# Four places back: a wait on an earlier landing for each opening load of a retention and feed-forward kernel

## The chip, the cores and the metric

The kernel runs on one core of one Trainium2 chip. The metric is the device time of one execution in microseconds (us), as the median of several runs. A core has TensorE (PE, the matmul engine), VectorE (DVE), ScalarE (ACT), GpSimd (POOL) and SyncE (SP). Each has its own queue and works it off in order; SP computes nothing here and issues most of the transfers. Sixteen DMA engines, shared by all queues, move data between the chip's memory (DRAM) and the core's on-chip memory.

## The reference

A recurrent retention layer over 4 batches, 8 heads, 768 positions and a head width of 64 feeds a two-layer perceptron:

```python
for t in range(S):
    state = gamma * state + outer(k[t], v[t])      # per batch and head, 64 x 64
    y[t] = scale * (q[t] @ state)
x = y, with the heads side by side                 # [3072, 512]
h = x @ w_in                                       # w_in [512, 2048]
g = max(h, 0) + alpha * min(h, 0)
out = g @ w_out                                    # w_out [2048, 512]
```

The decay gamma is a constant of each head. Inputs and output are float32.

## The kernel before

The kernel does the recurrence in chunks. A window w is 256 positions of four heads, and `place(w)` gives its batch, heads and positions; for each window k, q and v are loaded as tiles `ks`, `qs` and `vs` of 128 partitions by 512 elements, 256 KB each. `prep` scales k and q by powers of the decay into fp16 (`kdq`, L211, on DVE for the first windows and on POOL for later ones), `turn` transposes them on PE and copies them with ACT (L259, L265), `scores` and `masked` make the products within a chunk and mask them, `state_sums` makes the sums k·v that go into the state (L312), and `finish` writes the retention's output, transposed, into `xT`. v is cast to fp16 into `vx`, by ACT (L248) or POOL (L246).

The feed-forward part works on blocks of 512 positions. `ffn1` multiplies `xT` by w_in, in halves of 256 positions at first (L763) and then in wholes (L783); ACT and DVE apply the activation (L736, L725). `ffn2` multiplies by w_out (L809). Both weights come in pieces of 256 KB through the same buffers as k, q and v: `fetch` issues the load (L183) and `cast_w` casts a piece to fp16 on POOL (L188). In the first block, `tick` advances `ffn1` by a few matmuls at a time between the steps of the retention.

The whole order is written out by hand (a manual schedule): the order of the calls is the order on each engine, and waits are derived from which tile an instruction reads or overwrites. `behind(later, earlier, why)` adds a wait by hand.

What matters here is the opening, L1025 to L1089. ACT issues two small transfers (`tab`, 48 KB, and `alpha`, 8 KB). SP issues everything else in this order:

1. k and q of window 0, k and q of window 1, v of window 0, k and q of window 2, v of window 1, k and q of window 3, v of window 2 (L1027, eleven loads through L152);
2. the first piece of w_in, then v of window 3, then eleven more pieces of w_in (L1029 to L1033);
3. after the opening's instructions: the last four pieces of w_in, k, q and v of windows 4 and 5 among the sixteen pieces of w_out, and further windows.

The loads of 1 and 2 are 24 in number, go to buffers that nothing has used yet, and so wait for no other engine. The one thing that a load waits for is the counter that tells of landings: the build gives the DMAs eight counters in turn, so a load waits for the one eight places back in the list of all DMAs.

On POOL the order is: the scalings of windows 1 (q), 2 and 3, the cast of v of window 2, w_in's first piece, the cast of v of window 3, then the other pieces of w_in as they come, the scalings of window 4, and the pieces of w_out. On PE the opening begins with matmuls on a tile of ones (`busy`, L239, the `fill` of `turn` and `scores`) that compute nothing that is used.

Of the kernel before, what the change touches and what calls it, by code (L numbers as in the profile page):

```python
# [19 lines left out]
def kernel(  # L20
# [16 lines left out]
    nc = tc.nc  # L37
# [88 lines left out]
    def behind(later, earlier, why):  # L126
        tc.add_manual_dep(
            later.ins,
            earlier.ins.name,
            mybir.DependencyInfo(mybir.DependencyClass.Sync, mybir.DependencyReason.DATA),  # L130
            reason=why,
        )
# [7 lines left out]
    def place(w):  # L140
        u, g = divmod(w, 2)
        b, c3 = divmod(u, NUS)
        return u, g, b, c3

    def load(w, which="kqv"):
        u, g, b, c3 = place(w)
        t = staged.setdefault(w, {})
        for nm in which:
            src = {"k": k, "q": q, "v": v}[nm]
            t[nm] = sbp.tile([128, 4, 2 * D], FP, tag=f"{nm}s", bufs=8, name=f"{nm}s{w}")  # L150
            if w < NPE:
                nc.sync.dma_start(  # L152
                    out=t[nm],
                    in_=src[b, 4 * g : 4 * g + 4, TU * c3 : TU * c3 + TU, :].rearrange(
                        "h (p a) d -> p h (a d)", a=2
                    ),
                )
            else:
                at = TU * c3 + 128 * g
                nc.sync.dma_start(  # L160
                    out=t[nm].rearrange("p a (b d) -> p (a b) d", b=2),
                    in_=src[b, :, at : at + 128, :].rearrange("h p d -> p h d"),
                )
# [3 lines left out]
    def fetch(which, i, j):  # L167


        nm = "kqv"[len(pieces) % 3]  # L170
        t = sbp.tile([128, 4, 2 * D], FP, tag=f"{nm}s", bufs=8, name=f"{which}{i}_{j}")
        t = t.rearrange("p a b -> p (a b)")
        if which == "wo":
            src, dst = wo[:, 4 * i + j, :], w_out_all[:, 4 * i + j, :]
        elif i:
            s = slice(512 * i, 512 * i + 512)
            src, dst = wi[:, j, s], w_in_all[:, j, s]
        else:
            x, y = divmod(j, 2)
            at = slice(2 * y, 2 * y + 2), slice(256 * x, 256 * x + 256)  # L180
            src, dst = wi[:, at[0], at[1]], w_in_all[:, at[0], at[1]]
            t = t.rearrange("p (a b) -> p a b", a=2)
        nc.sync.dma_start(out=t, in_=src)  # L183
        pieces[which, i, j] = dst, t

    def cast_w(which, i, j):
# [800 lines left out]
    def tick(gen, m):  # L987
# [4 lines left out]
    wi = moe_w_in.rearrange("(hp p) d -> p hp d", p=128)  # L992
# [4 lines left out]
        out=ident,  # L997
        in_=ident,
# [6 lines left out]
    for i in range(2):  # L1005
        rows = slice(64 * i, 64 * i + 64)
        nc.gpsimd.affine_select(
            out=mask[rows].rearrange("p (a b j) -> p a b j", a=2, b=2),
            in_=ones[rows, 0:256].rearrange("p (a b j) -> p a b j", a=2, b=2),
# [7 lines left out]
            out=mask64[rows],  # L1017
            in_=ones[rows, 0:64],
# [6 lines left out]
    nc.scalar.dma_start(out=tab, in_=tab_h.ap())  # L1025
    nc.scalar.dma_start(out=alpha_sb, in_=moe_alpha.rearrange("(ft p) -> ft p", p=128))
    for w, which in ((0, "kq"), (1, "kq"), (0, "v"), (2, "kq"), (1, "v"), (3, "kq"), (2, "v")):  # L1027
        load(w, which)
    for i in range(3):  # L1029
        for j in range(4):  # L1030
            fetch("wi", i, j)
            if (i, j) == (0, 0):
                load(3, "v")  # L1033
    nc.vector.memset(warm, 0.0)
    nc.vector.memset(word, 0.0)
    nc.scalar.activation(out=warm, in_=warm, func=RELU, bias=0.0, scale=-1.0)
# [11 lines left out]
        out=oma_sb, in0=aps[:, 0:NFT], scalar1=-1.0, scalar2=1.0, op0=MULT, op1=ADD  # L1048
# [41 lines left out]
    for j in range(4):  # L1090
        fetch("wi", 3, j)
    load(4, "kq")
    for i in range(4):
        if i == 1:
            load(5, "kq")
        for j in range(4):
            if (i, j) == (1, 3):
                load(5, "v")
            fetch("wo", i, j)
        if i == 0:  # L1100
            load(4, "v")
# [14 lines left out]
    held = []  # L1116
# [115 lines left out]
```

## Time and profile before

| what | value |
|---|---|
| median of 3 runs | 199.52 us (198.75 to 199.85) |
| the profiled execution | 199.03 us, span 197.3 us |
| granted TensorE clock | 1.0 |
| PE busy | 191.6 us, 97% of the span |
| DVE, POOL, ACT busy | 76%, 58%, 50% |
| transfers, whole span | 38.21 MB, mean 194 GB/s |
| share of the chain that ended last by SP's queue and DMA | 4% and 3% |

The span is what the profiler saw between the first and the last instruction; the device time has some 1.7 us more around it. The page also cuts the span into 40 slices of 4.93 us. In the first nine slices, 44 us, the DMA engines are busy nearly throughout (the digits are tenths, the second row is what was moved):

```profile
DMA  5999999998899966999999999931072010400014
GB/s 163 318 345 371 357 348 382 402 343 186 192 215 232 238 154 157 317 325 233 219 178 230 240 322 236 219 75 41 3 212 56 0 56 3 161 0 3 0 56 159
```

A load's time to landing is counted from the start of its issue on SP to the moment at which all its DMA engines have told the counter that their part is there.

### The profile page before, as it was taken

To read this page: it belongs to the slowest core of one execution; us is meant where nothing else is said; L and a number is where in the kernel's file an instruction comes from. 1 tells how busy PE (TensorE), PEld (TensorE's weight loads), DVE (VectorE), ACT (ScalarE), POOL (GpSimd) and SP (SyncE) were. 2 spreads that over 40 slices of the span, in tenths; PEclk is the share of its full clock that TensorE was granted. 3 is DMA by queue.
4 is the path that set the end of the run, shared out by engine and by line. 5 is a ranking of instruction groups with operands and counts; after the bars stand their busy time and mean duration, and the time that the engine had idled before them with its cause. 6 is when DMAs were issued, how large, how long until landed. Compare 5 with 4: busy or idle time off the path is not lost.

```text
span 197.3 us, 6153 instructions
## 1 busy us (share of the span) xinstructions
PE 191.6 (97%) x2555; PEld 124.6 (63%) x2555; DVE 150.1 (76%) x251; ACT 97.9 (50%) x167; POOL 114.6 (58%) x153
## 2 busy tenths in 40 slices
PE   6989999999999999999999999999999999999993
PEld 2666545556885455444788644798544888448892
DVE  2585888564889956998995788995988964788962
ACT  3585765336686232477543276443376352566310
POOL 3489895856699991579892499381492091400011
PEclk9999999999999999999999999999999999999999
DMA  5999999998899966999999999931072010400014
GB/s 163 318 345 371 357 348 382 402 343 186 192 215 232 238 154 157 317 325 233 219 178 230 240 322 236 219 75 41 3 212 56 0 56 3 161 0 3 0 56 159
DMA packets 90476, 38.21 MB, mean 194 GB/s; under 512 B 68288, under 2 KB 85840, under 8 KB 90448
## 3 DMA queue, kind: packets, MB, share of 16 engines
q1 hardware_dynamic: 89856, 37.43, 71.5%
q8 instruction: 20, 0.33, 0.7%
q10 hardware_dynamic: 592, 0.39, 0.7%
q14 instruction: 8, 0.07, 0.1%
HBM read 27.32 MB, written 6.29 MB: 170 GB/s over the span
## 4 chain that ended last, share of the span: by engine, by line
PE 90%; SPq 4%; DMA 3%; issue 0%; POOL 0%; DVE 0%
PE hps L783 35%; PE ops L892 25%; PE ops L809 14%; PE hps L763 7%; SPq L152 4%; DMA vs<-in_v_dram 3%; PE y L614 2%; PE sc L638 1%; PE sums L652 1%; PE y L590 1%; PE trb L259 1%; PE y L392 1%; PE y L372 0%; PE sc L455 0%; SPq L183 0%
## 5 line engine op out<-in xcount | busy, mean ns | idle before, releaser
L725 DVE SCALAR_TENSOR_TENSOR gt<-hm,oma,hps 128x512 f16<-128x512 f32 (+1 forms) x112 | 73.0, 670 | 12.6 <-ACT hm L736 4.8
L736 ACT ACTIVATE hm<-hps 128x512 f32<-128x512 f32 x96 | 57.2, 597 | 32.5 <-PE hps L783 28.7
L783 PE MATMUL hps<-xT,win 128*128 128x512 f16 (+1 forms) x340 | 70.3, 366 | 0.0
L783 PEld LDWEIGHTS <-win 128*128 128x128 f16 x340 | 33.2, 98 | 35.2 <-DVE gt L725 0.4
L809 PE MATMUL ops<-wout,gt 128*128 128x512 f16 x128 | 29.3, 379 | 0.0
L913 POOL TENSOR_TENSOR c<-c,u 128x512 f32<-128x512 f32 x4 | 5.1, 1273 | 40.1 <-ACT c L908 22.1
L892 PEld LDWEIGHTS <-s 128*128 128x128 f16 x272 | 25.1, 98 | 2.8
L201 POOL TENSOR_TENSOR kdq<-ks,tab 128x256 f16<-128x256 f32 x32 | 19.0, 618 | 11.3 <-DMA ks<-in_k_dram 9.7
L948 POOL TENSOR_TENSOR s<-gt,s 128x1024 f16<-128x1024 f16 x6 | 13.8, 2310 | 13.1 <-PE sums L652 9.0
L892 PEld LDWEIGHTS <-gt 128*128 128x128 f16 x192 | 18.5, 98 | 2.9
L809 PEld LDWEIGHTS <-gt 128*128 128x128 f16 x128 | 11.9, 98 | 13.2
L201 POOL TENSOR_TENSOR kdq<-qs,tab 128x256 f16<-128x256 f32 x32 | 19.5, 632 | 0.0
L892 PE MATMUL ops<-wout,s 128*128 128x256 f16 (+1 forms) x136 | 15.3, 266 | 0.0
L892 PE MATMUL ops<-wout,gt 128*128 128x256 f16 x128 | 15.3, 273 | 0.0
L763 PE MATMUL hps<-xT,win 128*128 128x256 f16 x128 | 15.2, 273 | 0.0
L892 PE MATMUL ops<-t,s 128*128 128x256 f16 (+1 forms) x136 | 14.6, 266 | 0.0
L695 DVE TENSOR_TENSOR m<-sc,mi 128x1024 f16<-128x1024 f32 x8 | 9.8, 1220 | 4.7 <-PE sc L638 4.7
L763 PEld LDWEIGHTS <-win 128*128 128x128 f16 x128 | 12.0, 98 | 2.0
L828 ACT ACTIVATE os<-ops 128x512 f32<-128x512 f32 x8 | 4.7, 596 | 16.0 <-PE ops L809 14.7
L188 POOL CAST wout<-wo 128x512 f16<-128x512 f32 x16 | 10.5, 672 | 2.8 <-DMA wo<-in_moe_w_out_dram 2.7
L265 ACT ACTIVATE kq<-trb 128x512 f16<-128x512 f16 (+1 forms) x12 | 8.6, 736 | 4.8 <-PE trb L259 4.7
L231 POOL CAST vx<-vs 128x512 f16<-128x512 f32 x16 | 10.2, 639 | 0.6 <-DMA vs<-in_v_dram 0.6
(93 smaller groups left out, 217.7 us busy)
## 6 DMA issues: line engine op xcount, KB each, us to landing
ks<-in_k_dram SPq DMA_DIRECT2D x24, 256.0 KB, 4.6
qs<-in_q_dram SPq DMA_DIRECT2D x24, 256.0 KB, 4.6
vs<-in_v_dram SPq DMA_DIRECT2D x24, 256.0 KB, 4.5
wi<-in_moe_w_in_dram SPq DMA_DIRECT2D x16, 256.0 KB, 5.5
wo<-in_moe_w_out_dram SPq DMA_DIRECT2D x16, 256.0 KB, 5.5
out_dram<-c SPq DMA_DIRECT2D x11, 256.0 KB, 2.3
out_dram<-os SPq DMA_DIRECT2D x8, 256.0 KB, 3.9
out_dram<-y SPq DMA_DIRECT2D x3, 256.0 KB, 3.4
```

Source lines behind the costliest of these rows:

```text
L188: nc.gpsimd.tensor_copy(out=dst, in_=t)
L201: eng.tensor_tensor(out=kdq[:, kind, 2 * i : 2 * i + 2].rearrange("p x r d -> p r x d"), in0=src[:, 2 * i : 2 * i + 2].rearrange("p r (x d ...
L231: nc.gpsimd.tensor_copy(out=vx, in_=v_in)
L265: nc.scalar.activation(out=kq.rearrange("p b i -> p (b i)")[:, cols], in_=trb[:, cols], func=COPY, bias=0.0, scale=1.0,)
L695: nc.vector.tensor_tensor(out=m2.rearrange("p (s i) -> p s i", i=64), in0=sc.rearrange("p (s i) -> p s i", i=64), in1=mask64.unsqueeze(1). ...
L725: nc.vector.scalar_tensor_tensor(out=gt[:, ft, lo : lo + hps.shape[1]], in0=hm, scalar=oma_sb[:, ft : ft + 1], in1=hps, op0=MULT, op1=ADD,)
L736: nc.scalar.activation(out=hm, in_=hps, func=RELU, bias=0.0, scale=-1.0)
L763: nc.tensor.matmul(out=bank[:, 256 * x : 256 * x + 256], lhsT=w_in_all[:, hp, 128 * ft : 128 * ft + 128], rhs=tokens[:, hp // 2, 2 * t : 2 ...
L783: nc.tensor.matmul(out=hps[:, 128 * at.start : 128 * at.stop], lhsT=w_in_all[:, hp, 128 * ft : 128 * ft + 128], rhs=tokens[:, hp // 2, at, ...
L809: nc.tensor.matmul(out=opss[tq], lhsT=gt[:, ft, 128 * tq : 128 * tq + 128], rhs=w_out_all[:, ft, at], start=(ft == 0), stop=(ft == NFT - 1),)
L892: nc.tensor.matmul(out=banks[to][:, z : z + w], lhsT=left[:, kt % 4 if m == 3 else kt, 128 * t : 128 * t + 128], rhs=ts[m][:, kt, c : c + ...
L948: (nc.vector if last else nc.gpsimd).tensor_tensor(out=ss[3][i], in0=a12[:, cut], in1=ss[6][:, cut], op=SUB)
```

## The change

Each of the 24 loads of the opening is put in a list, `first`. From the fifth on, each gets a wait, by `behind`, on the landing of the load four places before it in that list: the loads of k, q and v through the new argument `held` of `load`, the pieces of w_in in `fetch`, up to the twelfth piece (`i < 3`). So that each load finds its own partner, L1027's pairs are loaded one tensor at a time, in the same order. Loads after w_in's twelfth piece get no such wait. The argument `on` isn't used.

```diff
-    def load(w, which="kqv"):
+    first = []
+
+    def load(w, which="kqv", on=None, held=None):
...
             if w < NPE:
-                nc.sync.dma_start(
+                ins = (on or nc.sync).dma_start(
                     out=t[nm],
...
                 )
+                if held is not None:
+                    behind(ins, held, "four loads are under way at a time")
+                first.append(ins)
...
-        nc.sync.dma_start(out=t, in_=src)
+        ins = nc.sync.dma_start(out=t, in_=src)
+        if which == "wi" and i < 3:
+            behind(ins, first[-4], "four loads are under way at a time")
+            first.append(ins)
         pieces[which, i, j] = dst, t
...
     for w, which in ((0, "kq"), (1, "kq"), (0, "v"), (2, "kq"), (1, "v"), (3, "kq"), (2, "v")):
-        load(w, which)
+        for nm in which:
+            load(w, nm, held=first[-4] if len(first) > 3 else None)
     for i in range(3):
         for j in range(4):
             fetch("wi", i, j)
             if (i, j) == (0, 0):
-                load(3, "v")
+                load(3, "v", held=first[-4])
```

In the built kernel the instructions of every engine and their order are the same as before; the waits of SP's loads differ, as told. The four pieces of w_in after the twelfth no longer wait for a counter by themselves, since the waits ahead of them already imply it.

## The prediction

> **What bounds the kernel now.** The shares of the chain that ended last come first: they say which engine sets the end.
>
> ```profile
> PE 90%; SPq 4%; DMA 3%; issue 0%; POOL 0%; DVE 0%
> ```
>
> TensorE (PE) sets nine tenths of it. The rest lies in the opening, so I read the same chain in order of time (start us, us, what) from 9.68 us on:
>
> ```profile
> 9.68 5.19 DMA vs<-in_v_dram
> ...
> 14.92 0.63 POOL vx L246
> ...
> 15.59 0.31 PE st L312 x8
> ```
>
> SP's queue issues one load after the other, the v of window 3 is issued at 9.68 and lands at 14.87, POOL casts it, and from 15.59 on the chain is PE alone. So a landing that moves before 15 us can move the end one for one; a landing after it counts only beyond its cover. Next the timeline of SP's queue:
>
> ```profile
> 0.80 0.45 SPq L152 DMA_DIRECT2D ks<-in_k_dram  x1
> ...
> 2.95 0.51 SPq L152 DMA_DIRECT2D vs<-in_v_dram  x1
> ...
> 4.12 1.09 SPq L152 DMA_DIRECT2D qs<-in_q_dram  x1
> 5.25 1.26 SPq L152 DMA_DIRECT2D vs<-in_v_dram  x1
> ```
>
> Six loads go out 0.5 us apart, then an issue itself takes over 1 us. Times to landing, asked for one issue at a time, at 0.80, 1.32 and 2.95 (last column us):
>
> ```profile
> ks<-in_k_dram SPq DMA_DIRECT2D x1, 256.0 KB, 2.9
> ```
> ```profile
> qs<-in_q_dram SPq DMA_DIRECT2D x1, 256.0 KB, 3.3
> ```
> ```profile
> vs<-in_v_dram SPq DMA_DIRECT2D x1, 256.0 KB, 5.1
> ```
>
> Issue plus landing gives 3.70, 4.65 and 8.05; the k of window 1, issued at 1.85 and landing after 4.7, gives 6.55, and w_in's twelfth piece, issued at 16.85 and landing after 5.6, gives 22.45. Landings come in the order of the issues: one queue, first come first served. Whether the engines behind it ever starve is read from the windows (last two columns: DMA share, GB/s):
>
> ```profile
> 4.00:6.50 2.50, 2.50 (x15) 1.62 (x14) 1.20 (x2) 0.60 (x1) 0.00 (x0) 1.00 0.96 264
> 6.50:9.00 2.50, 2.50 (x36) 1.55 (x34) 1.86 (x3) 1.51 (x3) 1.17 (x2) 1.00 1.15 346
> ...
> 15.00:18.00 3.00, 2.88 (x64) 1.88 (x63) 1.47 (x3) 1.08 (x3) 2.85 (x5) 1.00 1.06 397
> ```
>
> They don't: from 6.5 us on the share stays over 1, and there is one dip, 264 GB/s between 4.0 and 6.5. The 5 us to landing is mostly queueing.
>
> **The change, part by part.** Of the 24 opening loads the first four are untouched and twenty get a wait on the landing four places back. Nothing is moved: the order on SP stays, no computing instruction is added, and the wait replaces one that was mostly already met (in the built kernel a load waits for the counter used eight DMAs back). An instruction that waits costs the queue next to nothing: the chain shows 0.05 us from vs's landing (14.87) to its cast (14.92). Behind the waiting load on SP stand only later loads, up to w_in's fourth block and the w_out pieces; SP computes nothing.
>
> *What gets later.* The fifth load (v of window 0) goes out at 3.75 instead of 2.95, the sixth at 4.70 instead of 3.50. In a served-in-order queue an issue that is late costs nothing as long as it reaches the engines before its turn. So I work out each landing as the later of two: the landing before it plus one service, or the landing four back plus 0.05 plus A, the time from issue to landing without a queue. Service: 262,144 B at 346 GB/s is 0.76 us for q, k, v, at 397 GB/s 0.66 us for w_in. A is not shown with three loads ahead. Its lower bound is 2.9, the first load, with nothing ahead. Above it are 3.3 (the second load) and 3.6 (a q issued at 117.90 right behind one k, far from the opening), the upper bound. I take 2.9, since the queueing is in the other term and 3.3 has some of it in.
>
> With A = 2.9: four services of 0.76 are 3.04 against 2.95, so the wait never decides for q, k, v. The fifth lands at the later of 7.30 + 0.76 and 3.70 + 2.95, that is 8.06 (before 8.05); the seventh at 9.5 by both terms; the thirteenth (v of window 3) at 14.9 as before. For w_in four services are 2.64, so the wait decides every fourth: w_in's fifth piece at 14.88 + 2.95 = 17.83 (17.4 before), the ninth at 20.78 (20.05), the twelfth at 22.8, or 23.3 if the stall of 0.5 us before its tenth piece comes again (22.45 before). That is 0.3 to 0.8 us late at the end of the stretch, and as the queue stays full afterwards the w_out pieces inherit it.
>
> *What covers it.* Start and length of the casts and of the matmuls that read them, asked in narrow windows:
>
> ```profile
> 19.49 0.62 POOL L188 CAST win<-wi 128x512 f16<-128x512 f32 x1
> ```
> ```profile
> 20.85 0.59 PE L783 MATMUL hps<-xT,win 128*128 128x512 f16 x2
> ```
> ```profile
> 33.38 1.63 POOL L188 CAST wout<-wo 128x512 f16<-128x512 f32 x2
> ```
> ```profile
> 34.70 0.59 PE L809 MATMUL ops<-wout,gt 128*128 128x512 f16 x2
> ```
>
> w_in's eighth piece is cast by 20.11 and first read by the second of that pair, at 21.07: 0.96 us of cover. w_in's twelfth: cast by 23.14, read at 24.52, 1.38 us. The thinnest cover is further on: w_out's sixth piece, the second of the casts from 33.38, is ready at 34.45 and read at 34.92, 0.47 us. If that cover is gone, PE stalls by the rest. So 0.3 to 0.8 us late costs 0 to 0.33 us; I take 0.1.
>
> *What may get earlier.* The dip cost (346 − 264) × 2.5 / 346 = 0.6 us of transfer. In it five or six loads were under way and issues took 1.09 and 1.26 us. If the crowd made the dip, four under way take it away and all landings after it come up to 0.6 us sooner. On PE that is worth less: before 15.59 it waited 0.50 us for POOL's k of window 3 (whose load landed late) and 0.39 for a copy by ACT, and the rest of the time it ran. Bounds: nothing, and 0.6 us. From 6.5 on the same six are under way at 346 GB/s, so the crowd alone is not the cause; I take 0.1.
>
> **Sum.** 0.1 − 0.1 = 0 on the profiled execution's own 199.03 us (span 197.3 and 1.7 around it). That run lies 0.5 us under the median of 199.52; I forecast the median: 199.5.
>
> One rule speaks against the change. The Trainium skill ("DMA: Bandwidth & Descriptors", Rules for kernel authors) says to issue a DMA early and wait late, so that its fixed cost overlaps; waiting on every fourth landing exposes that cost. The same page (Anatomy of one DMA) puts it at about 2.0 us plus bytes over 436 GB/s, fitted on the GpSimd path: for this load an estimate of 2.6 us, 0.3 under the row. With 2.6 the wait would never decide a q, k, v landing and hardly a w_in one, and the sum would be −0.1 instead of 0.
>
> **The rivals.**
>
> *Slower: the round trip outlasts four services.* If A is 3.3, the same two terms give: seventh 6.55 + 3.35 = 9.9 (9.5), eleventh 13.25 (12.6), thirteenth 14.8 to 15.6 (14.88, the later figure if the jump of 0.9 us before it stays), w_in's fifth 18.1 to 18.95, twelfth 23.5 to 24.3, 1.05 to 1.85 us late, less the cover of 0.47: +0.6 to +1.4 us, 200.5 at the middle. With A = 3.6 the twelfth comes at some 24.9, 2.45 late, +2.0, 201.5. It decides from A of about 3.0, where 4 × 0.76 is less than A + 0.05 and q, k, v come late too. For it: a load takes the slowest of 16 engines, and each new wait adds up their stalls instead of letting the others run ahead. Against it: three loads are still queued at each landing, 2.3 us of work. This is also how the skill's rule would come out.
>
> *Faster: the dip was the crowd.* −0.5 us by the bound above, 199.0. If POOL's chain of scalings (1.04 us each from 7.42 on, back to back but for 0.41, 0.24 and 0.60 us of waiting for loads) starts earlier too, PE, ACT and POOL give up at most these 1.25 us: 198.3. For it: the slow issues stand exactly in the dip. Against it: see above.
>
> *The wait is empty.* If it hardly delays an issue, nothing changes at all; it shows as the fifth issue staying at 2.95. The time is the forecast's, so it is counted there.
>
> **How the numbers follow.** No change, between 198.9 and 200.1: 0.58. Slower rival: 0.23. Faster rival: 0.19. A measurement of this kernel (three runs from 198.75 to 199.85) tells about 0.5%, 1 us, from no change. Of the slower rival 0.20 passes that (its middle lies on it and its tail is long), and 0.02 of the forecast's weight: slower 0.22. The faster one passes it only if POOL's waits go as well, to which I give 0.13, and 0.01 comes from the forecast: faster 0.14. The rest is the same: 0.64. The range: down to 198.5, short of the faster rival's end, and up to 201.0, past the slower one's middle.
>
> **What would show it.** Right: the fifth load issued at 3.7 to 3.8; landings spaced by 0.75 us; v of window 3 landing at 14.5 to 15.2, with about 3 us from issue to landing instead of 5; PE alone on the chain from about 15.6. Wrong towards slower: landings in groups of four with gaps of over 3.1 us from group to group, DMA share under 1 between 7 and 20 us, and PE waiting for POOL's weight casts at L783 or L809. Wrong towards faster: over 330 GB/s between 4.0 and 6.5 us, the k of window 1 landing near 5.5 instead of 6.55, and PE's state sums of window 3 before 15.1.

## The result: slower by 2.9%, and the profile after

| | before | after |
|---|---|---|
| median of 6 runs | 199.69 us (198.75 to 200.9) | 205.14 us (204.17 to 206.91) |
| ratio, 95% interval | | 1.0285 (1.0246 to 1.0325) |
| the profiled execution, span | 199.03, 197.3 us | 205.91, 204.2 us |

The ratio and its interval leave out executions over 1.5% above the fastest of their kernel, which count as slow. The predicted time of 199.5 us and the range up to 201.0 were wrong. The slower rival's side was the right one, but the loss of 5.5 us is more than five times its middle price (+1.0 us) and nearly three times its highest (+2.0). The shares of the chain that ended last, after:

```profile
PE 72%; DMA 24%; POOL 2%; issue 0%; DVE 0%; SPq 0%
```

Transfers went from 3% to 24%, and SP's queue from 4% to nothing. The same chain up to the point from which PE alone is on it, in order of time (start us, us, what):

```profile
0.80 2.90 DMA ks<-in_k_dram
...
3.72 3.51 DMA vs<-in_v_dram
...
7.29 3.80 DMA ks<-in_k_dram
...
11.11 4.92 DMA vs<-in_v_dram
...
16.04 4.57 DMA wi<-in_moe_w_in_dram
...
20.64 4.95 DMA wi<-in_moe_w_in_dram
...
26.05 7.26 DMA ks<-in_k_dram
...
35.43 5.80 DMA wo<-in_moe_w_out_dram
...
41.29 5.11 DMA wo<-in_moe_w_out_dram
...
48.19 5.34 DMA vs<-in_v_dram
...
54.25 0.32 PE sums L483 x16
```

Each of the first six links is one load, and the next link is the load four places on, issued 0.02 us after the landing. Up to 25.6 us the added waits are the chain. A link was to last 2.95 us at most times; it lasts 3.5 to 5 after the first. The last four links are loads without an added wait, of later windows and of w_out. They make nearly half of the 24%, 23.5 us against 24.7. PE alone is on the chain from 54 us on; in the kernel before it was from 15.6. Next SP's timeline (start us, length us), which is also a list of landings, since each issue from the fifth on stands 0.01 to 0.08 us behind one:

```profile
3.72 0.37 SPq L154 DMA_DIRECT2D vs<-in_v_dram  x1
4.54 0.37 SPq L154 DMA_DIRECT2D ks<-in_k_dram  x1
5.76 0.37 SPq L154 DMA_DIRECT2D qs<-in_q_dram  x1
6.50 0.37 SPq L154 DMA_DIRECT2D vs<-in_v_dram  x1
7.29 0.37 SPq L154 DMA_DIRECT2D ks<-in_k_dram  x1
8.71 0.37 SPq L154 DMA_DIRECT2D qs<-in_q_dram  x1
```

The issue itself now takes 0.33 to 0.37 us where six in the kernel before took 0.65 to 1.26. The shorter queue is the likely reason, which was not tested by itself. Window 1 lands 0.8 us sooner than before in this execution (its k at 5.68 instead of 6.51). After that the issues come 0.7 to 1.4 us apart, one us on the mean. The windows of after (last three columns: granted PE clock, DMA share, GB/s) show what that does:

```profile
4.00:6.50 2.50, 2.50 (x15) 1.55 (x14) 1.88 (x3) 0.60 (x1) 0.00 (x0) 1.00 1.03 306
6.50:9.00 2.50, 2.36 (x34) 1.55 (x33) 1.28 (x2) 1.93 (x4) 1.29 (x2) 1.00 0.96 290
...
15.00:18.00 3.00, 2.19 (x56) 1.46 (x55) 1.71 (x3) 0.34 (x2) 2.55 (x5) 0.75 0.70 205
18.00:21.00 3.00, 3.00 (x37) 1.58 (x36) 0.24 (x2) 1.19 (x2) 1.24 (x3) 0.50 0.81 249
21.00:24.00 3.00, 3.00 (x22) 2.20 (x22) 1.56 (x4) 1.20 (x2) 1.76 (x4) 0.61 0.69 154
```

The dip between 4.0 and 6.5 us is partly filled (306 instead of 264 GB/s), but from 6.5 on the DMA engines have less to do: a share of 0.7 to 0.96 where it had been over 1, and 154 to 290 GB/s where it had been 340 to 400. By the trace's landings w_in's twelfth piece, the last load with an added wait, comes at 27.9 us instead of 22.5, 5.4 us late. Behind it the lateness still grows: w_out's sixth piece, the one whose cover the prediction found thinnest, lands at 40.6 instead of 33.0, 7.6 us late. This execution is 6.9 us longer than the profiled one of the kernel before. PE pays for it in its waits (us, times, longest), here for casts of w_in:

```profile
PEld L791 <- POOL win L196: 2.1, 3, 1.1
```

There is a second loss in these windows, the granted clock of 0.50. It gets an experiment of its own.

### The profile page after: what moved, and what is told of

It is laid out like the page before. It is cut to its first block, busy times and chain, and to the rows that moved or that the text cites. A ratio compares the mean times of both kernels' runs of the same rounds, so it can differ in the third digit from the quotient of the medians.

```text
span 204.2 us, 6151 instructions
## 1 busy us (share of the span) xinstructions
PE 195.6 (96%) x2555; PEld 125.6 (62%) x2555; DVE 150.1 (73%) x251; ACT 98.3 (48%) x167; POOL 113.9 (56%) x153
## 4 chain that ended last, share of the span: by engine, by line
PE 72%; DMA 24%; POOL 2%; issue 0%; DVE 0%; SPq 0%
PE hps L791 29%; PE ops L900 24%; PE ops L817 8%; DMA ks<-in_k_dram 7%; DMA vs<-in_v_dram 7%; DMA wo<-in_moe_w_out_dram 5%; PE hps L771 5%; DMA wi<-in_moe_w_in_dram 5%; PE y L622 1%; PE sums L660 1%; PE sc L646 1%; PE y L598 1%; POOL kdq L219 1%; POOL wout L196 1%; POOL vx L254 0%; PE y L400 0%
## 5 line engine op out<-in xcount | busy, mean ns | idle before, releaser
L733 DVE SCALAR_TENSOR_TENSOR gt<-hm,oma,hps 128x512 f16<-128x512 f32 (+1 forms) x112 | 73.0, 670 | 15.6 <-ACT hm L744 8.2
L791 PEld LDWEIGHTS <-win 128*128 128x128 f16 x340 | 33.1, 98 | 36.7 <-POOL win L196 2.1
L771 PE MATMUL hps<-xT,win 128*128 128x256 f16 x128 | 17.5, 297 | 0.0
L771 PEld LDWEIGHTS <-win 128*128 128x128 f16 x128 | 12.9, 105 | 3.0 <-issue 0.2
L196 POOL CAST win<-wi 128x512 f16<-128x512 f32 x16 | 9.8, 616 | 7.3 <-DMA wi<-in_moe_w_in_dram 7.1
L196 POOL CAST wout<-wo 128x512 f16<-128x512 f32 x16 | 9.7, 616 | 3.3 <-DMA wo<-in_moe_w_out_dram 3.0
```

The costliest lines, as they stand in the source:

```text
L196: nc.gpsimd.tensor_copy(out=dst, in_=t)
L733: nc.vector.scalar_tensor_tensor(out=gt[:, ft, lo : lo + hps.shape[1]], in0=hm, scalar=oma_sb[:, ft : ft + 1], in1=hps, op0=MULT, op1=ADD,)
L771: nc.tensor.matmul(out=bank[:, 256 * x : 256 * x + 256], lhsT=w_in_all[:, hp, 128 * ft : 128 * ft + 128], rhs=tokens[:, hp // 2, 2 * t : 2 ...
L791: nc.tensor.matmul(out=hps[:, 128 * at.start : 128 * at.stop], lhsT=w_in_all[:, hp, 128 * ft : 128 * ft + 128], rhs=tokens[:, hp // 2, at, ...
```

## The experiments

All are the changed kernel with one thing altered, except w4_again, which is the changed kernel itself, and the last, which is the kernel before with one thing altered. Three theories were set against each other. *Round trip*: four loads are too few to fill the time from issue to landing. *The wait as such*: each stop and start of the queue has a price. *The clock*: PE stands, its clock is halved, and that is the loss.

**How many places back.** The wait looks six, five, three places back, or one. A helper picks the landing; the 6 becomes 5, 3 or 1:

```diff
+    def back():
+        n = len(first)
+        return first[n - 6] if n >= 6 and True else None
...
-            behind(ins, first[-4], "four loads are under way at a time")
+            if back() is not None:
+                behind(ins, back(), "a window of loads")
...
-            load(w, nm, held=first[-4] if len(first) > 3 else None)
+            load(w, nm, held=back())
```

> The wait is on the landing six places back instead of four; 18 loads wait. Round trip theory: in the changed kernel a load took 3.5 to 4.1 us from issue to landing for k, q, v and 4.2 to 5.0 for most of w_in with four under way, and four services of 0.76 and 0.66 us are less than that; six services are 4.56 and 3.96, so k, q, v land as before the change and w_in 0 to 0.5 us later, which is covered: within 0.7 us of the kernel before (199.7). Price of the wait as such (a queue that stops and starts again loses time at each of the waits, however many loads are under way): 18 of 20 waits, so nearly the whole loss stays, 204 to 205. Clock theory (the loss is the half clock from 16 us on): 200 to 203, with the clock at half again if PE stands as long as it did.

> Five places back. Round trip theory: five services are 3.8 and 3.3 us against a round trip of about 3.7 and 4.2, so k, q, v just keep up and w_in comes every 0.84 us instead of 0.66, some 2 us late at its twelfth piece less 0.5 of cover: 200.3 to 202.5. Price of the wait as such: 204 to 205.5. Clock theory: as with four, if PE stands; 203 to 205.

> Three places back. Round trip theory: a landing every 1.1 to 1.25 us for k, q, v and 1.2 to 1.4 for w_in, w_in's twelfth piece at 30 to 34 us instead of 22.5 before the change: 207 to 212. Price of the wait as such: 21 waits instead of 20, as the changed kernel, 205 to 206. Clock theory: the half clock lasts longer, 206 to 209.

> Each load waits for the one before it, so that its time from issue to landing is that of a load alone. It measures A, which was taken as 2.9: by the row it was taken from, 2.6 to 2.9 us for k, q, v and about the same for w_in, and w_in's twelfth piece lands at some 65 us. If a load alone takes 2.6 to 2.9, then the 3.5 and more with four under way is queueing and the spread of the 16 engines; if it takes 3.4 or more, A was simply too small. Time about 240 us in either case.

Landings of the 13th load (v of window 3) and the 24th (w_in's twelfth piece) are from each trace. The ratio of four places back is to its own runs of the kernel before, 199.69 us; the others are to 199.91:

| places back | waits | 13th, 24th landing, us | time, us | ratio to before (95%) |
|---|---|---|---|---|
| none (before) | | 14.9, 22.5 | 199.91 | |
| six | 18 | 15.1, 23.4 | 200.04 | 1.0019 (0.999 to 1.0049) |
| five | 19 | 14.7, 24.9 | 202.05 | 1.0112 (1.0059 to 1.0165) |
| four (the change) | 20 | 16.0, 27.9 | 205.14 | 1.0285 (1.0246 to 1.0325) |
| three | 21 | 17.2, 32.5 | 212.56 (one run) | 1.063 |
| one | 23 | 37.0, 68.6 | 246.85 (one run) | 1.235 |

18 waits cost nothing measurable, 20 cost 5.5 us: the wait as such has no price, and that theory falls. The round trip theory's ranges hold for six and five places back; three came out 0.6 us over its upper end.

Landing and loss belong together within one execution. From six places back down to one, w_out's sixth piece is 2.0, 4.4, 7.6, 13.2 and 48.0 us later than in the kernel before. The profiled executions are 1.9, 3.2, 6.9, 13.5 and 47.8 us longer than the profiled one before (six's is the slowest of its ten). The 24th landing is only 1.0, 2.4, 5.4, 10.0 and 46.1 us late. So 1 to 3 us of the lateness arise behind the last added wait; what makes them was not separated.

The run with one place back gives the disputed price alone. It was expected at about 240 us with its 24th landing at some 65; both came higher. SP's timeline of that kernel, each issue being the landing before it plus 0.02 us:

```profile
6.68 0.37 SPq L158 DMA_DIRECT2D ks<-in_k_dram  x1
9.55 0.37 SPq L158 DMA_DIRECT2D qs<-in_q_dram  x1
12.24 0.37 SPq L158 DMA_DIRECT2D vs<-in_v_dram  x1
15.04 0.37 SPq L158 DMA_DIRECT2D ks<-in_k_dram  x1
```

A load of k, q or v alone takes 2.7 to 2.9 us (the very first one 3.0): the value taken, 2.9, was right. A w_in piece of the first block took 2.45 us, of the second and third 3.0 to 3.1. With four under way the same loads took these times (last column):

```profile
ks<-in_k_dram SPq DMA_DIRECT2D x1, 256.0 KB, 3.8
```
```profile
vs<-in_v_dram SPq DMA_DIRECT2D x1, 256.0 KB, 5.3
```

(issued at 7.29 and 9.44). So the loads that share the queue add 1 us and more, although the queue is short. Counting the trace's packets shows how short. When a load with an added wait is issued, three others are nominally under way; with four places back, in the calm stretch from 5.8 to 12 us, only 1.7 to 2.3 loads of these are still to be moved, 1.3 to 1.7 us of work at 0.76. (Six places back: 3.8 of five; three: 1.2 to 1.6 of two.) The rest has been moved, but has not all been told: a landing is the last of sixteen steps of its counter, one from each DMA engine, and in this stretch the last comes 0.7 to 1.3 us after the first (alone, 0.35 to 0.65 us). The first packet of the first load started 1.2 us after its issue. That an engine ahead of the others runs dry between the two is an inference: the trace doesn't name the engine of a packet. What one late engine does to the others is looked at below.

**Which loads.** The wait is kept for a part of them only. The helper's last line in the three kernels (the comments are not in them):

```python
return first[n - 4] if n >= 4 and n < 13 else None    # waits_kqv: 5th to 13th load
return first[n - 4] if n >= 4 and n > 12 else None    # waits_win: 14th to 24th load
return first[n - 4] if n >= 4 and n < 8 else None     # first_four: 5th to 8th load
```

> Four places back as in the change, but only for the 5th to the 13th load (k, q, v and w_in's first piece); w_in's later eleven pieces have no added wait. Round trip theory: v of window 3 lands near 16 us as in the changed kernel (14.9 before), then the queue fills up again and w_in comes every 0.66 us, its twelfth piece at some 23.5 us; PE's opening is 1.2 to 1.8 us late: 200.7 to 202. If the loss were all made here: 204 to 206. Clock theory: half clock from 16 us on as in the changed kernel, another 1 to 3 us on top: 202 to 205.

> Four places back, but only for the last eleven pieces of w_in (14th to 24th load); k, q and v as before the change. Round trip theory: with 4.2 to 4.6 us from issue to landing, a piece every 1.05 to 1.15 us, the twelfth at 26.5 to 27.5 us instead of 22.5, less 0.5 of cover: 202.8 to 204.5, the larger part of the loss. Clock theory: PE doesn't stand before 15 us, so the clock stays whole and the loss is small: 199.7 to 201.

> Four places back, but only for the 5th to the 8th load. Round trip theory: in the changed kernel the first eight loads land at or before the times of before (k and q of window 1 at 5.7 and 6.5 instead of 6.5 and 7.3), so nothing is lost, and POOL begins 0.75 us sooner: 199.2 to 200.0. Crowd theory (the dip between 4 and 6.5 us comes from six loads under way): the dip is filled in part, and the 13th load lands up to 0.6 us sooner: 199.2 to 199.6.

waits_kqv: 201.81 us, ratio 1.013 (1.0088 to 1.0173). waits_win: 203.87 us, 1.0236 (1.0189 to 1.0282). Both lie where the round trip theory put them; w_in's stretch carries the larger part. In the profile of waits_win the granted clock is 1.0, and it still loses 2.4%; in that of waits_kqv it is at half from 18.1 to 21.5 us, and the loss is the smaller one.

first_four missed: 200.8 us, 1.008 (1.0047 to 1.0113), where at most 200.0 was expected. The profiled execution, 199.89, is one of its faster ones, so it shows a part of that loss at most. Its windows:

```profile
4.00:6.50 2.50, 2.08 (x16) 1.07 (x15) 1.78 (x3) 0.72 (x2) 0.00 (x0) 1.00 0.92 273
6.50:9.00 2.50, 2.28 (x43) 1.53 (x44) 1.60 (x3) 1.76 (x4) 1.54 (x2) 1.00 0.89 263
9.00:12.00 3.00, 2.72 (x82) 1.87 (x81) 2.08 (x5) 1.61 (x5) 1.99 (x3) 1.00 1.06 307
```

The dip is hardly smaller (273 against 264 GB/s) and is followed by a new one, 263 and 307 where the kernel before has 346 and 340. Four waits are enough to shorten the queue: when the 5th to 8th load are issued, 1.6 to 2.1 loads are still to be moved, in the kernel before 3.4 to 4.0, and 3.8 is reached again only at the 13th issue. The 13th landing is 15.9 instead of 14.9, but free_1k below, without added waits and without a loss in its median, has one at 15.65 in its trace. So a late 13th landing is not the waits' alone, and where the 1.6 us go isn't settled. The crowd theory's gain, a 13th landing up to 0.6 us sooner, did not come.

**The clock.** The page's row of the granted clock, after (tenths, 40 slices of the span):

```profile
PEclk9996799999999999999999999999999999999999
```

In the profiled execution PE ran at half clock from 16.5 to 23.3 us (the expectation below is half a microsecond early), after this wait of PE (in brackets; the longest after its first matmul):

```profile
15.44 0.22 PE L320 MATMUL st<-vx,kdq 64*64 64x64 f16 x3 [1.25 <-POOL vx L254]
```

The experiment gives PE something to do there:

```diff
     finish(1)
-    state_sums(2, (0,))
+    at = ps("st0", "p")
+    busy(24, at)
+    state_sums(2, (0,), at)
```

> The changed kernel, with six more matmuls on the tile of ones (512 columns each, 1.3 us) on PE just before window 2's state sums, where PE stood for 1.25 us in the changed kernel; their result is not used. Clock theory: PE no longer stands, the half clock from 16.0 to 22.9 us does not come, and 2 to 4 us come back: 201 to 203. Round trip theory: the loads land as late as before, PE waits for w_in's casts instead of running slowly, and at most 1 us comes back: 204 to 205.3.

Measured: 204.74 us (204.06 to 205.22), ratio 1.0267 (1.0213 to 1.032), where the round trip theory put it. In the profiled execution the clock stayed whole, and the first half-block matmuls finished sooner, as PE's timelines of the changed kernel and of this one show for the same twenty:

```profile
21.19 3.38 PE L771 MATMUL hps<-xT,win 128*128 128x256 f16 x20
```
```profile
19.28 2.36 PE L776 MATMUL hps<-xT,win 128*128 128x256 f16 x20
...
29.44 2.76 PE L796 MATMUL hps<-xT,win 128*128 128x512 f16 x12 [1.63 <-POOL win L201]
```

1.9 us earlier at their start, and then PE waits for w_in's casts, 4.8 us in all on its weight loads instead of 2.1:

```profile
PEld L796 <- POOL win L201: 4.8, 5, 1.9
```

So the half clock was mostly hidden behind the late loads. PE's busy time says the same: 195.6 us in the changed kernel, 193.4 here with 1.5 us of added matmuls, so that 3.7 us of slower running came back as waiting. Of six runs of the changed kernel the two with the clock nearly whole (0.998 and 0.999) took 204.17 and 204.48, the two with 0.983 took 205.8 and 205.91. But the two with 0.99 took 204.41 and 206.91, so six runs don't give the clock's price. It is no cause of the rest: waits_win and w5 lose 2.4% and 1.1% with the clock whole in their profiles.

**Why w_in suffers most.** SP's timeline of the changed kernel has three gaps in that stretch, from 12.47 to 14.73, from 17.64 to 20.01 and from 21.88 to 23.72. Into the first two falls a 16 KB packet of the instruction queue, at 12.55 and 17.2 us (0.9 and 1.3 us long in the trace; the kernel before has such packets too, at 12.68 and 18.75). The changed kernel was run again, beside one with w_in's later blocks cut like the first, in runs of 1 KB:

```diff
-        elif i:
-            s = slice(512 * i, 512 * i + 512)
-            src, dst = wi[:, j, s], w_in_all[:, j, s]
         else:
             x, y = divmod(j, 2)
-            at = slice(2 * y, 2 * y + 2), slice(256 * x, 256 * x + 256)
+            at = slice(2 * y, 2 * y + 2), slice(512 * i + 256 * x, 512 * i + 256 * x + 256)
```

> The changed kernel once more, beside the next run on the same chip, and for a second profile: 204.2 to 206, landings of k, q, v every 0.9 to 1.0 us on the mean and of w_in every 1.0 to 1.1, gaps of about 2 us where a 16 KB packet of the instruction queue or a bunch of slow packets falls into the stretch, each gap followed by another one four loads later.

> The changed kernel with w_in's second and third block (and the fourth) in pieces of the first block's shape: two row blocks by 256 columns, runs of 1 KB instead of 2 KB. Alone, a piece of the first block took 2.45 us to land and one of the second or third 3.0. If that price of the shape sets the pace of the w_in stretch under four, eight pieces save 0.55 us each over four under way, 1.1 us: 203.8 to 204.6. If the pace is set by what happens when several loads share the 16 engines (stalls of single engines that all then wait for), the shape matters little: within 0.6 us of the run beside it.

w4_again: 204.97 us as the median of three runs, 1.0318 (1.0257 to 1.0378); a fourth, the profiled one, took 208.18. The landings of that one show gaps over 2 us for the 11th, 16th and 20th load, the last exactly four after the one before it. w4_1k: 204.05 us, 1.0263 (1.0209 to 1.0317). The medians are 0.9 us apart, on the side of a price of the shape, but the intervals overlap: not settled. The same cut without any added wait:

> The kernel before (no added wait) with all of w_in in pieces of two row blocks by 256 columns, runs of 1 KB. With a full queue the shape's price alone is hidden: the DMA engines' rate decides, 346 to 397 GB/s, and w_in had 0.5 to 1.4 us of cover: same as before, within 0.4 us. If runs of 2 KB cost time with a full queue too, up to 0.5 us faster.

199.1 us, ratio 0.9984 (0.9959 to 1.001): no difference. With a full queue the shape's price is hidden. No kernel of the study beats the one before.

**One late engine, with and without the wait.** The counter's steps in the kept traces show what a stall of one DMA engine does. In the changed kernel fifteen of the sixteen steps of the 11th load had come by 13.11 us; the last came at 14.72. The 15th load waits for that landing and goes out at 14.73, when only 0.4 of a load is still to be moved. Taken by the middle of its sixteen steps, the 14th load, issued before the stall, is 1.1 us later than in the kernel before, and the 15th is 2.3 us later: not the one engine alone has lost the time. free_1k has the same kind of stall with no added wait. Fifteen steps of its 12th load had come by 13.37 us, the last at 15.00. That landing is late, and the execution took 200.26 us. But the loads behind it lose nothing: the middle step of the 24th load comes at 21.11 us, in the kernel before at 21.20.

## Why the prediction was wrong

*What bounds the kernel: right.* The landings of the opening and of the weights beyond their cover decided the time.

*The wait itself costs next to nothing: right.* SP goes on 0.02 us after a landing, and six places back is free with 18 waits.

*A of 2.9 us: right for a load alone* (2.7 to 2.9), and short by 0.1 to 0.2 for most of w_in.

*The step that failed* is the rule that takes "each landing as the later of two: the landing before it plus one service, or the landing four back plus 0.05 plus A". It treats 16 engines as one server that is never idle while loads are under way. A landing is that of the slowest engine, and a service of 0.76 us is the mean of all. In free_1k, with a full queue, the other engines ran on while one was 1.6 us late, and the loads behind lost nothing; in the changed kernel the same lateness set the issue of the next load for all of them. The prediction's remark that "three loads are still queued at each landing, 2.3 us of work" was the same error: the packets show 1.7 to 2.3 loads, 1.3 to 1.7 us, against 1.2 us from issue to first packet. The links measured 3.5 to 5 us instead of 2.95.

*The slower rival* had the mechanism ("each new wait adds up their stalls instead of letting the others run ahead") and got 0.23. Its price was too low because A was raised to 3.3 or 3.6 only and evenly; single gaps of about 2 us in w_in's stretch were not in it. The Trainium skill's rule ("DMA: Bandwidth & Descriptors", Rules for kernel authors) to issue early and wait late pointed the same way. The estimate of 2.6 us from the Trainium skill (the same page, Anatomy of one DMA) is close to the 2.7 of a load alone, and the conclusion drawn from it, that nothing would be lost, fails in the same step.

*The cover* of 0.47 us on w_out's sixth piece was about right: that piece came 7.6 us late and the execution was 6.9 us longer. The w_out pieces did inherit the lateness, as predicted, and 2.2 us beyond that of w_in's twelfth.

*The dip*: the landings of window 1 came 0.8 us sooner in the profiled execution, as the faster rival said, and this was given back by 9 us. It is no sure gain: in w4_again, the same kernel, the k of window 1 comes only 0.1 us sooner, and in waits_win, where these loads have no added wait, 0.5. The dip itself is 273 to 306 GB/s in the six traces with four back on the first loads, 263 to 270 in the three without added waits there. What made it is open; six places back it stands at 276 GB/s.

*The clock* was not thought of. It is no large part of the loss.

Open: how w_in's longer landings divide among the shape of its runs, the instruction packets and bunches of slow packets. In five traces (the changed kernel twice, w6, first_four and free_1k) a step that comes 1.0 to 1.7 us after the other fifteen stands 2.1 to 2.6 us behind the start of the first such packet, with added waits and without. That the packet makes it was not tested.

## What to carry to other kernels

To bound the loads under way, compare two times that the trace gives: the work still queued when the issue is let go, and the time from an issue to its first packet. Here four loads of 256 KB left about 1.5 us against 1.2 us, and one engine's stall held up the other fifteen; six left 2.9 us and cost nothing measurable. A time to landing of 5 us that is mostly queueing was no waste here: the order was right, and cutting the queue didn't bring the data sooner.

## What the runs showed of the hardware that was not expected

A load of 256 KB from runs of 2 KB (w_in's later blocks) takes 3.0 us alone, one from runs of 1 KB 2.45 and one from runs of 512 B (k, q, v) 2.7 to 2.9. One engine's part of a load came up to 1.8 us after the other fifteen (w3). The granted PE clock fell to half at 16.5 us, for 6.8 us, after a stretch in which PE's longest wait was 1.25 us; it was busy for 2.05 of the 3.42 us before the fall. w6 was busy for 2.29 us of the same stretch and kept its clock, so what decides is not shown. The Trainium skill ("TensorE: Matmul & The Clock Gate", Part 1: The HAM clock gate) speaks of an idle window of about 3.4 us before that happens; here no wait was that long.
